# A retention layer feeding a PReLU MLP: another creation order of the early operations

## The chip, the cores and the metric

The kernel runs on one core of a Trainium2 chip. A core has five engines that run side by side and wait for each other through semaphores: TensorE (PE; its weight loads are shown as PEld), VectorE (DVE), ScalarE (ACT), GpSimd (POOL) and SyncE (SP), whose queue here issues the DMA transfers. The metric is the device time of one execution in microseconds (us). Times are medians over runs. The profile is one execution taken by the hardware profiler; its span runs from the first to the last instruction.

## What is computed

```python
def _attn_ref(q, k, v):                      # 8 batches, 8 heads, 576 rows, 64 columns
    scores = scale * np.matmul(q, k.transpose(0, 1, 3, 2))
    gamma = 1.0 - 2.0 ** (-5.0 - np.arange(H, dtype=np.float32))
    rel = pos[:, None] - pos[None, :]
    Dmat = np.where(rel >= 0, gamma[:, None, None] ** rel[None, :, :], 0.0)
    return np.matmul(scores * Dmat[None], v)
...
def _moe_ref(x, w_in, w_out, alpha):         # x is 4608 x 512, w_in 512 x 2048, w_out 2048 x 512
    h = x @ w_in
    g = np.maximum(h, 0.0) + alpha * np.minimum(h, 0.0)
    return g @ w_out
```

The output of the first function, heads side by side, is `x` of the second. The weights arrive as 64-bit words (the kernel reads them as pairs of 32-bit integers) and are converted to float32 on the chip.

## The kernel before

**Retention.** Rows of a batch are cut into 9 chunks of 64. Within a chunk the masked scores are formed; what earlier chunks contribute goes through a state of 64 x 64 per head. The first two batches are worked in *parts* of 4, 4 and 1 chunks over all heads: parts 0, 1, 2 are batch 0, parts 3, 4, 5 are batch 1. A part is loaded (`load_part`: k, q, v rows, 256 KB per 128 rows), q and v are scaled on POOL (`part_scale`, L455), k and q are turned on PE and copied out by ACT (`part_transposes`, L479, L485), scores are formed and masked (`part_scores`, L503, L510), states are summed (`part_states`, L526, L541), carried to the next part on POOL (`part_carry`, L547), and values are formed from scores (L574) and states (L599, in part 0 L615) and copied to the `x` tiles (L631). The one-chunk parts go through `last_part` (L652 turns k and q, L665 to L691 the rest). Later batches are worked as head pairs: `joint_(n)` issues the score and state products of pair n (L913 to L923) together with the values of pair n-1 (L861), and the loads and scalings of the next ones.

**MLP.** `x` stands in 18 blocks of 256 rows, the hidden width in 8 units of 256. A *visit* is a block with four units. The first two visits (8 *cells*: block 0 or 1 with units 0 to 3) run as plain float32 products: `unit_plain` (L1091, then L1097, L1102 for the PReLU) and `second_plain` (L1122). Later visits run on operands split in three pieces each (`split_roll`, `split_w`, `split_g`): `unit_roll` (L1188) and `second` (L1340) in the *rolling steps* s = 0 to 14, each with two units i of two halves f, and from the last blocks on `unit_two` (L1222).

**Weights.** `weights(n)` fetches the next n of the 16 early weight pieces (512 KB each), converts them (ACT L730, L732; DVE L740, L742, L751; POOL L754) and leaves them in the `lx_w` rooms, from which the plain units read them. Unit u reads pieces 4u and 4u+1, its second product pieces 4u+2 and 4u+3. The cells are numbered so that block 0 and 1 take units 0 and 1 first; cells 0 and 1 therefore use pieces 0 to 7. `split_w(i)` later splits piece i into the three planes for the rolling steps (L783, L785, L790).

**Order.** Nothing is issued at once. Every call of `do` or `dma` appends an operation with its engine, an estimated cost, its dependencies and the buffers that it takes. *Creation order* decides which use of a buffer comes before which, and so some dependencies, and breaks ties; PE operations are also picked only from a stretch of 150 in creation order. At the end `dues` works out from behind how late each operation may be, `plan` lists the operations forward, engine by engine, and a loop of 243 random shifts of the due times keeps what `plan` rates best. The instructions are then issued in that planned order, and each engine and queue runs its own in order.

During the first 100 us of the plan at most 1.25 MB of transfers are allowed in flight on SP's queue (`IN_FLIGHT`).

**Unread products.** `fill` (L1405) issues products of the identity into a bank that nobody reads: 5 at the start, 3 more behind part 0's first transposes, and 10 after part 0's values, each float32 product being two records in the trace.

## Time and profile before

| | |
|---|---|
| median of 3 runs | 919.32 us (918.11 to 922.28) |
| span of the profiled execution | 917.4 us |
| instructions | 19097, of which PE 7289 products |
| granted TensorE clock | 1.000 |
| largest group | second products of the rolling steps, L1340, 1392 records in 338.8 us |
| HBM | 74.19 MB read, 32.51 MB written |

A row of the profile names the line, the engine, the operation, the tiles it writes and reads, the shapes and how many instructions are merged. In rows of a timeline the first two numbers are the start in the span and the time to the end of the group; the bracket is the idle time of the engine before the group and what ended it. A matmul's end is modelled and overlaps its successor, so distances are better read from start to start.

### The profile page before, as it was taken

Reading aid. Unit: us, or ns where it says so; the run is one execution under the profiler, and the core shown is the slowest. Engines: PE = TensorE matmul, PEld = TensorE weight load, DVE = VectorE, ACT = ScalarE, POOL = GpSimd, SP = SyncE. Lnnn points to the kernel's source line nnn. Section 1 sums busy time; section 2 is a strip of 40 time slices with the busy share of each in tenths; the row PEclk is TensorE's granted clock in tenths of the full one; section 3 lists DMA queues with packets and bytes.
Section 4 is the critical chain, followed back from the end, with each engine's and each line's share of the span. In section 5 each row is a group of like instructions: output and inputs, shape, how many; then the busy total and the mean of one; then the engine's idle time right before and its main releaser. Section 6 shows DMA issues by size and latency. Waiting matters only on the chain. (4 is left out here: it accounts for less than half of the span.)

```text
span 917.4 us, 19097 instructions
## 1 busy us (share of the span) xinstructions
PE 906.9 (99%) x7289; PEld 737.8 (80%) x7289; DVE 548.0 (60%) x1003; ACT 503.9 (55%) x1010; POOL 520.2 (57%) x461
## 2 busy tenths in 40 slices
PE   7999999999999999999999999999999999999998
PEld 6767688887888888888888888888888888888886
DVE  5786766667677667676757776344444534344343
ACT  4575455646565656565746555537463636364441
POOL 4776746456466665674542244665656656574624
PEclk9999999999999999999999999999999999999999
DMA  9995688977988879895243332212121322211112
GB/s 216 251 235 86 164 189 186 198 178 155 221 192 194 209 166 201 193 189 181 93 138 130 102 125 65 86 57 81 58 89 56 99 73 86 74 64 47 47 46 69
DMA packets 235947, 121.32 MB, mean 132 GB/s; under 512 B 203456, under 2 KB 203728, under 8 KB 235856
## 3 DMA queue, kind: packets, MB, share of 16 engines
q1 hardware_dynamic: 235712, 119.98, 52.1%
q8 instruction: 57, 0.93, 0.4%
q14 instruction: 34, 0.28, 0.1%
q10 hardware_dynamic: 144, 0.13, 0.0%
HBM read 74.19 MB, written 32.51 MB: 116 GB/s over the span
## 5 line engine op out<-in xcount | busy, mean ns | idle before, releaser
L1340 PE MATMUL pso<-w,g 128*128 128x512 f32 x1392 | 338.8, 391 | 0.0
L1340 PEld LDWEIGHTS pso<-w,g 128*128 128x128 f32 x1392 | 258.9, 188 | 55.2 <-POOL g L1267 1.2
L1264 POOL TENSOR_TENSOR g<-ga_all,g 128x512 fp32r<-128x512 f32 x76 | 97.9, 1291 | 130.4 <-ACT g L1260 105.0
L1267 POOL TENSOR_TENSOR g<-g 128x512 fp32r<-128x512 f32 x114 | 147.4, 1294 | 23.7 <-DVE su L1066 5.7
L1188 PE MATMUL psh<-lx_x,w 128*128 128x512 f32 (+1 forms) x360 | 86.6, 379 | 0.0
L1188 PE MATMUL psa<-lx_x,w 128*128 128x512 f32 (+1 forms) x360 | 85.4, 376 | 0.0
L1188 PEld LDWEIGHTS psa<-lx_x,w 128*128 128x128 f32 x360 | 65.1, 188 | 13.1 <-issue 0.4
L1188 PEld LDWEIGHTS psh<-lx_x,w 128*128 128x128 f32 x360 | 64.2, 188 | 12.9
L1260 ACT ACTIVATE g<-ga_all 128x512 fp32r<-128x512 f32 x76 | 47.6, 631 | 43.0 <-PE pso L1340 21.0
L1256 POOL TENSOR_TENSOR g<-g 128x512 fp32r<-128x512 f32 x22 | 28.5, 1296 | 64.0 <-DVE g L1253 38.3
L1264 POOL TENSOR_TENSOR g<-vn,g 128x512 fp32r<-128x512 f32 x25 | 32.4, 1297 | 37.5 <-ACT g L1260 34.9
L1340 PE MATMUL pso<-lx_x,g 128*128 128x512 f32 x216 | 53.5, 390 | 0.1
L1163 POOL TENSOR_TENSOR lx_x<-lx_x 128x512 fp32r<-128x512 f32 x28 | 35.9, 1294 | 26.0 <-DVE lx_x L1160 26.0
L941 DVE SCALAR_TENSOR_TENSOR at<-psa,pf,mask 64x512 f32<-64x512 f32 x48 | 36.0, 749 | 21.1 <-PE psh L861 10.2
L1340 PEld LDWEIGHTS pso<-lx_x,g 128*128 128x128 f32 x216 | 40.4, 188 | 9.0 <-DVE o L1363 0.7
L1262 ACT ACTIVATE g<-ga_all 128x512 fp32r<-128x512 f32 x76 | 47.2, 621 | 0.0
L1358 DVE TENSOR_TENSOR op<-pso,op 128x512 f32<-128x512 f32 x35 | 24.0, 686 | 31.3 <-PE pso L1340 31.2
L1202 ACT COPY ga_all<-psh 128x512 f32<-128x512 f32 (+1 forms) x30 | 16.7, 558 | 39.1 <-PE psh L1188 37.4
L861 PEld LDWEIGHTS psh<-at,vn 128*64 128x64 f32 x864 | 27.9, 137 | 8.7 <-issue 3.6
L1222 PE MATMUL psh<-w,w 128*128 128x512 f32 x144 | 34.6, 389 | 0.0
L1222 PE MATMUL psa<-w,w 128*128 128x512 f32 x144 | 34.6, 389 | 0.0
L754 POOL TENSOR_TENSOR wa<-wa,op 128x512 int32<-128x512 int32 x16 | 21.0, 1311 | 23.1 <-DVE wa L751 19.1
(329 smaller groups left out, 1883.3 us busy)
## 6 DMA issues: line engine op xcount, KB each, us to landing
xk<-x SPq DMA_DIRECT2D x18, 512.0 KB, 3.7
ok<-o SPq DMA_DIRECT2D x36, 256.0 KB, 2.9
op<-ok SPq DMA_DIRECT2D x18, 512.0 KB, 3.9
out_dram<-o SPq DMA_DIRECT2D x35, 256.0 KB, 2.3
x<-xk SPq DMA_DIRECT2D x16, 512.0 KB, 5.6
qx<-in_q_dram SPq DMA_DIRECT2D x96, 72.0 KB, 3.4
kx<-in_k_dram SPq DMA_DIRECT2D x96, 72.0 KB, 3.3
kn<-in_k_dram SPq DMA_DIRECT2D x48, 144.0 KB, 3.4
```

What stands on the lines that cost most here:

```text
L861: nc.tensor.matmul(pv[i].get()[half(h2), (j - js[0]) * C:(j - js[0] + 1) * C], vns[n % 2][:, h2, j], mt.get()[:, h2, j], start=True, stop= ...
L941: nc.vector.scalar_tensor_tensor(out=mt.get()[half(1 - h2), h2, j], in0=fro[x], scalar=pf[x, 1, h:h + 1], in1=mask[x, None, :].to_broadcas ...
L1163: do("POOL", 1.29, lambda h=h, l=l, d=d: nc.gpsimd.tensor_tensor(out=piece(d()), in0=h(), in1=l(), op=ALU.subtract), [(g, 0, n), (g, 1, n) ...
L1188: nc.tensor.matmul(out_of(p), w[:, c0:c0 + P], xp(l, cc), start=(l != 1 and cc == 0), stop=(l > 0 and cc == NCC - 1))
L1222: nc.tensor.matmul(p.get(), w[:, c0:c0 + P], piece(words_of(g)[:, o:o + DM]), start=(l != 1 and cc == 0), stop=(l > 0 and cc == NCC - 1))
L1256: do("POOL", 1.29, lambda: nc.gpsimd.tensor_tensor(out=piece(to.get()[:, 2]), in0=to.get()[:, 0], in1=to.get()[:, 1], op=ALU.subtract), [( ...
L1260: do("ACT", 0.64, lambda: nc.scalar.mul(piece(to.get()[:, 2]), whole(), BELOW), both, [(to, 2)])
L1262: do("ACT", 0.64, lambda: nc.scalar.mul(piece(to.get()[:, 0]), whole(), BELOW * 2.0 ** -12), both, [(to, 0)])
L1264: do("POOL", 1.29, lambda: nc.gpsimd.tensor_tensor(out=piece(to.get()[:, 1]), in0=whole(), in1=to.get()[:, 2], op=ALU.subtract), both + [( ...
L1267: do("POOL", 1.29, lambda: nc.gpsimd.tensor_tensor(out=piece(to.get()[:, 2]), in0=to.get()[:, 0], in1=to.get()[:, 1], op=ALU.subtract), [( ...
L1340: nc.tensor.matmul(a[2 * m + b].get(), piece(g.get()[:, l, f, m * P:(m + 1) * P]), w_piece(u, 2 + f, l), start=(cell["first"] and f == 0 a ...
L1358: do("DVE", 0.69, lambda: nc.vector.tensor_tensor(out=t(), in0=p1.get(), in1=t(), op=ALU.subtract), [(p1, 0)], [tk])
```

## The change

What was a sequence of statements up to the first rolling step becomes a tuple `early` of small steps, called in turn, that also takes in the rolling steps 0 to 3. The loop for the rest starts at step `FIRST = 4` and makes the same calls as before. The same loads, parts, units, weight pieces, splits and joints are created, in another order:

- the 8 unread products at the start and behind the first transposes stand nearer to each other; the 10 ahead of the first plain unit are gone;
- weight pieces are asked for one by one between the steps of the parts; part 2 is loaded ahead of part 1, the alphas ahead of part 0's transposes, the first head pair's rows right after;
- part 0 goes in the order k's transposes, q's transposes, states, scores, values; `last_part(2)` stands ahead of the second products of cell 1;
- `split_w` of the 16 early pieces, all behind `joint_(8)` before, are spread from the middle of part 4 on; cells 4 and 5 exchange their second products; the second product of cell 7 comes after the first rolling half unit;
- block 3 is split ahead of block 2 in `split_roll`;
- dependencies of an operation are kept in creation order (`sorted`) instead of a set's.

```diff
-        op.deps = [d for d in deps if d is not op]
+        op.deps = sorted((d for d in deps if d is not op), key=lambda d: d.n)
...
-    EARLY, JOINTS = 1, {(s, i): 1 for s in range(14) for i in range(2) if (s, i) not in ((0, 0), (8, 1), (10, 1), (13, 0), (13, 1))}
+    FIRST, JOINTS = 4, {(s, i): 1 for s in range(14) for i in range(2) if (s, i) not in ((0, 0), (8, 1), (10, 1), (13, 0), (13, 1))}
...
-    load_part(0, ((0, 0), (1, 0), (1, 1), (0, 1), (2, 0), (2, 1)))
-    bank = banks_of(0)
-    fill(5, 0.43)
-    part_transposes(0, 0, bank)
-    fill(3, 0.43, [next(op for op in ops if op.eng == "PE" and len(op.deps))])
-    part_scale(0, 1)
-    part_transposes(0, 1, bank)
-    part_scores(0, bank)
-    part_scale(0, 2)
-    weights(3)
-    part_states(0, bank)
-    do("DVE", 2.0, tables, (), [(cst, "t")])
-    part_carry(0)
-    part_values(0, bank)
-    fill(10, 0.25, of_pe())
-    weights(1)
-    fetch_x(visits[0])
...
-    load_part(1)
-    bank = banks_of(1)
-    unit_plain(cells[0])
...
-    done.add(8)
-    joint_(8)
-    second_plain(cells[7])
-    for i in range(16):
-        split_w(i)
...
+    bank0, bank1 = banks_of(0), banks_of(1)
+    early = (
+        lambda: load_part(0, ((0, 0), (1, 0), (1, 1), (0, 1), (2, 0), (2, 1))),
+        lambda: fill(5, 0.43),
+        lambda: weights(1),
+        lambda: weights(1),
+        lambda: part_scale(0, 1),
+        lambda: fill(3, 0.43, of_pe()[:1]),
+        lambda: part_scale(0, 2),
+        lambda: load_part(2),
+        lambda: load_part(1),
+        lambda: alpha(),
+        lambda: part_scale(1, 1),
+        lambda: load_kq(8),
+        lambda: part_transposes(0, 0, bank0),
+        lambda: weights(1),
+        lambda: do("DVE", 2.0, tables, (), [(cst, "t")]),
+        lambda: part_transposes(0, 1, bank0),
+        lambda: part_states(0, bank0),
+        lambda: part_transposes(1, 1, bank1),
+        lambda: part_scores(0, bank0),
+        lambda: part_scale(1, 2),
+        lambda: part_values(0, bank0),
+        lambda: fetch_x(visits[0]),
+        lambda: weights(1),
+        lambda: part_scale(2, 1),
+        lambda: part_transposes(1, 0, bank1),
+        lambda: weights(1),
+        lambda: part_scores(1, bank1),
+        lambda: unit_plain(cells[0]),
+        lambda: part_carry(0),
+        lambda: weights(1),
+        lambda: weights(1),
+        lambda: second_plain(cells[0]),
+        lambda: part_states(1, bank1),
+        lambda: part_carry(1),
+        lambda: unit_plain(cells[1]),
+        lambda: part_values(1, bank1),
...
+        lambda: last_part(2),
+        lambda: second_plain(cells[1]),
+        lambda: unit_plain(cells[2]),
+        lambda: unit_plain(cells[3]),
...
+        lambda: split_roll(visits[3]),
+        lambda: split_w(12),
+        lambda: split_roll(visits[2]),
+        lambda: next_joint(),
+        lambda: unit(0, 0, 0),
+        lambda: pump(1),
+        lambda: second_plain(cells[7]),
+        lambda: unit(0, 0, 1),
...
+        lambda: next_split(6),
+    )
+    for step in early:
+        step()
+    land[0] = LAND[1]
+    for s in range(FIRST, last):
+        begin(s)
...
```

In the new list `bank0` and `bank1` are two generators over the same PSUM banks as before, `unit(s, i, f)` makes one half of a rolling unit, `next_split` and `next_joint` call `split_roll` and `joint_`, and `swap` gives the `lx` rooms their second use.

More of the change, by code (lines that the diff above doesn't have):

```diff
@@ L1425 @@
-    fill(10, 0.25, of_pe())
-    weights(1)
-    fetch_x(visits[0])
-    dma(lambda: a16, lambda: moe_alpha.rearrange("(t p) -> t p", p=P), NFC * P * 4, (), [(cst, "al")])
-    aps = Gen(psa[0])
-    do("PE", 0.2, lambda: nc.tensor.transpose(aps.get()[:, 0:NFC], a16, ident[0:NFC, 0:NFC]), [(cst, "al")],
-       [(aps, 0)])
-    do("DVE", 0.1, lambda: nc.vector.tensor_scalar(malpha, aps.get()[:, 0:NFC], -1.0, 1.0,
-                                                   ALU.mult, ALU.add), [(aps, 0)], [(cst, "a")])
@@ L1434 @@
-    load_part(1)
-    bank = banks_of(1)
-    unit_plain(cells[0])
-    weights(2)
-    part_transposes(1, 0, bank)
-    part_scale(1, 1)
-    part_transposes(1, 1, bank)
-    second_plain(cells[0])
-    weights(2)
-    part_scale(1, 2)
-    part_scores(1, bank)
-    part_states(1, bank)
-    unit_plain(cells[1])
-    load_part(2)
-    part_values(1, bank)
-    part_carry(1)
-    fetch_x(visits[1])
-    part_scale(2, 1)
-    part_scale(2, 2)
-    rooms(3)
-    load_part(3)
-    second_plain(cells[1])
@@ L1456 @@
-    unit_plain(cells[2])
-    last_part(2)
-    weights(2)
-    for x in (4, 5):
-        rooms(x)
-    part_transposes(3, 0, bank)
-    part_scale(3, 1)
-    part_transposes(3, 1, bank)
-    second_plain(cells[2])
-    part_scores(3, bank)
-    part_scale(3, 2)
-    part_states(3, bank)
-    part_carry(3)
-    unit_plain(cells[3])
-    part_values(3, bank)
-    load_part(4)
-    weights(2)
-    second_plain(cells[3])
-    part_transposes(4, 0, bank)
-    part_scale(4, 1)
-    part_transposes(4, 1, bank)
@@ L1477 @@
-    unit_plain(cells[4])
-    load_part(5)
-    weights(2)
-    second_plain(cells[4])
-    part_scores(4, bank)
-    part_scale(4, 2)
-    part_states(4, bank)
-    part_carry(4)
-    unit_plain(cells[5])
-    part_values(4, bank)
-    load_kq(8)
-    load_kn(8)
-    load_v(8)
-    weights(2)
-    second_plain(cells[5])
-    part_scale(5, 1)
-    part_scale(5, 2)
-    unit_plain(cells[6])
-    last_part(5)
-    operands(8)
-    load_kq(9)
-    load_v(9)
-    second_plain(cells[6])
-    unit_plain(cells[7])
@@ L1501, with alpha @@
-    done.add(8)
-    joint_(8)
-    second_plain(cells[7])
-    for i in range(16):
-        split_w(i)
+    def alpha():
+        dma(lambda: a16, lambda: moe_alpha.rearrange("(t p) -> t p", p=P), NFC * P * 4, (), [(cst, "al")])
+        aps = Gen(psa[0])
+        do("PE", 0.2, lambda: nc.tensor.transpose(aps.get()[:, 0:NFC], a16, ident[0:NFC, 0:NFC]),
+           [(cst, "al")], [(aps, 0)])
+        do("DVE", 0.1, lambda: nc.vector.tensor_scalar(malpha, aps.get()[:, 0:NFC], -1.0, 1.0,
+                                                       ALU.mult, ALU.add), [(aps, 0)], [(cst, "a")])
@@ L1507, with swap @@
+    def swap():
+        was_in = lxs[0].gen.ops + lxs[1].gen.ops
+        for x in lxs:
+            x.gen = None
+        lxs[:] = lx_slots("x")
+        for x in lxs:
+            Gen(x).before = was_in
     ready_kb = [((kb + 1) * TB - 1) // S for kb in range(NKB)]
-    todo = iter(range(2 * NPAIR + 1, len(pairs) + 1))
+    todo = iter(range(2 * NPAIR, len(pairs) + 1))
+    done.add(2 * NPAIR)
     of = {}
@@ L1610, in take_rooms, with slow, g, begin @@
             lambda f: rows[:, :, f * TB:(f + 1) * TB] if len(cs) == 2 else rows[:, 0, f * TB:(f + 1) * TB])
-    was_in = lxs[0].gen.ops + lxs[1].gen.ops
-    lxs[:] = lx_slots("x")
-    for x in lxs:
-        Gen(x).before = was_in
-    for _ in range(EARLY):
-        joint_(next(todo))
-    land[0] = LAND[1]
-    split_roll(visits[2])
-    last = singles - 1
-    t = 8
-    for s in range(last):
+    last = singles - 1
+    t = [8]
+    plan_of, held_rooms = {}, {}
+    def slow(f):
+        def g(*a):
+            was, land[0] = land[0], LAND[1]
+            f(*a)
+            land[0] = was
+        return g
+    def begin(s):
         some = [visits[kb] for kb in (1 + s, 2 + s) if 2 <= kb <= last]
@@ L1625, with unit @@
         now_cells = {(vis["n"], u): c for vis in some for c in of[vis["n"]] for u in us if c["u"] == u}
-        queue += [now_cells[vis["n"], u] for vis in some for u in us]
+        queue.extend(now_cells[vis["n"], u] for vis in some for u in us)
+        plan_of[s] = sorted(some, key=lambda vis: vis["kb"] % 2), us, now_cells
+    @slow
+    def unit(s, i, f):
         quick[0] = s >= QUICK
-        by_side = sorted(some, key=lambda vis: vis["kb"] % 2)
-        if s == 0:
-            split_roll(visits[3])
@@ L1631 @@
-        for i, u in enumerate(us):
-            cs = [now_cells[vis["n"], u] for vis in by_side]
-            gens, g = take_rooms(cs)
-            for f in range(2):
-                for _ in range(ahead.get(t, 0)):
-                    convert((op_, 0), was, None)
-                t += 1
-                ps = unit_roll(by_side, u, f, True)
-                acts_roll(ps, gens, g, u, f)
-                if f:
-                    for c, ga in zip(cs, gens):
-                        c["ga"] = ga, ga.get
-                    ahead_g()
-                pump(PUMP_R[i][f])
-                if f:
-                    for _ in range(JOINTS.get((s, i), 0)):
-                        joint_(next(todo))
-                if i and f and 3 + s <= last and s:
-                    assert NPAIR * (ready_kb[3 + s] + 1) in done
-                    split_roll(visits[3 + s])
+        by_side, us, now_cells = plan_of[s]
@@ new lines, in unit, with next_split @@
+        cs = [now_cells[vis["n"], us[i]] for vis in by_side]
+        if not f:
+            held_rooms[s, i] = take_rooms(cs)
+        gens, g = held_rooms[s, i]
+        for _ in range(ahead.get(t[0], 0)):
+            convert((op_, 0), was, None)
+        t[0] += 1
+        ps = unit_roll(by_side, us[i], f, True)
+        acts_roll(ps, gens, g, us[i], f)
+        if f:
+            for c, ga in zip(cs, gens):
+                c["ga"] = ga, ga.get
+            ahead_g()
+    @slow
+    def next_split(s):
+        assert NPAIR * (ready_kb[s] + 1) in done
+        split_roll(visits[s])
@@ new lines, in next_joint @@
+    @slow
+    def next_joint():
+        joint_(next(todo))
+    bank0, bank1 = banks_of(0), banks_of(1)
[36 more added lines that the diff above has]
+        lambda: part_values(1, bank1),
+        lambda: rooms(3),
+        lambda: weights(1),
+        lambda: fetch_x(visits[1]),
+        lambda: load_part(3),
+        lambda: rooms(4),
+        lambda: part_scale(2, 2),
+        lambda: last_part(2),
+        lambda: second_plain(cells[1]),
+        lambda: unit_plain(cells[2]),
+        lambda: unit_plain(cells[3]),
+        lambda: rooms(5),
+        lambda: part_transposes(3, 0, bank1),
+        lambda: weights(1),
+        lambda: part_scale(3, 2),
+        lambda: part_states(3, bank1),
+        lambda: load_part(5),
+        lambda: part_scale(3, 1),
+        lambda: load_part(4),
+        lambda: part_transposes(3, 1, bank1),
+        lambda: begin(0),
+        lambda: part_scale(4, 1),
+        lambda: part_carry(3),
+        lambda: weights(1),
+        lambda: weights(1),
+        lambda: weights(1),
+        lambda: weights(1),
+        lambda: part_scale(4, 2),
+        lambda: part_scores(3, bank1),
+        lambda: part_transposes(4, 1, bank1),
+        lambda: part_values(3, bank1),
+        lambda: part_transposes(4, 0, bank1),
+        lambda: part_states(4, bank1),
+        lambda: second_plain(cells[2]),
+        lambda: part_scores(4, bank1),
+        lambda: weights(1),
+        lambda: unit_plain(cells[4]),
+        lambda: split_w(7),
+        lambda: second_plain(cells[3]),
+        lambda: part_values(4, bank1),
+        lambda: load_kn(8),
+        lambda: load_v(8),
+        lambda: weights(1),
+        lambda: operands(8),
+        lambda: part_scale(5, 2),
+        lambda: unit_plain(cells[5]),
+        lambda: second_plain(cells[5]),
+        lambda: split_w(6),
+        lambda: part_scale(5, 1),
+        lambda: split_w(13),
+        lambda: load_kq(9),
+        lambda: load_v(9),
+        lambda: second_plain(cells[4]),
+        lambda: split_w(10),
+        lambda: unit_plain(cells[6]),
+        lambda: next_joint(),
+        lambda: split_w(5),
+        lambda: weights(1),
+        lambda: second_plain(cells[6]),
+        lambda: split_w(2),
+        lambda: part_carry(4),
+        lambda: split_w(1),
+        lambda: split_w(11),
+        lambda: split_w(14),
+        lambda: split_w(9),
+        lambda: split_w(3),
+        lambda: split_w(0),
+        lambda: unit_plain(cells[7]),
+        lambda: last_part(5),
+        lambda: split_w(4),
+        lambda: split_w(8),
+        lambda: swap(),
+        lambda: split_roll(visits[3]),
+        lambda: split_w(12),
+        lambda: split_roll(visits[2]),
+        lambda: next_joint(),
+        lambda: unit(0, 0, 0),
+        lambda: pump(1),
+        lambda: second_plain(cells[7]),
+        lambda: unit(0, 0, 1),
+        lambda: pump(1),
+        lambda: unit(0, 1, 0),
+        lambda: split_w(15),
+        lambda: pump(1),
+        lambda: unit(0, 1, 1),
+        lambda: next_joint(),
+        lambda: pump(1),
+        lambda: begin(1),
+        lambda: unit(1, 0, 0),
+        lambda: pump(1),
+        lambda: unit(1, 0, 1),
+        lambda: next_joint(),
+        lambda: pump(1),
+        lambda: unit(1, 1, 0),
+        lambda: pump(1),
+        lambda: unit(1, 1, 1),
+        lambda: pump(1),
+        lambda: next_joint(),
+        lambda: next_split(4),
+        lambda: begin(2),
+        lambda: unit(2, 0, 0),
+        lambda: pump(1),
+        lambda: unit(2, 0, 1),
+        lambda: pump(1),
+        lambda: next_joint(),
+        lambda: unit(2, 1, 0),
+        lambda: pump(1),
+        lambda: unit(2, 1, 1),
+        lambda: pump(1),
+        lambda: next_joint(),
+        lambda: next_split(5),
+        lambda: begin(3),
+        lambda: unit(3, 0, 0),
+        lambda: pump(1),
+        lambda: unit(3, 0, 1),
+        lambda: next_joint(),
+        lambda: pump(1),
+        lambda: unit(3, 1, 0),
+        lambda: pump(1),
+        lambda: unit(3, 1, 1),
+        lambda: next_joint(),
+        lambda: pump(1),
+        lambda: next_split(6),
+    )
@@ L1651 @@
+    for step in early:
[3 more added lines that the diff above has]
+        begin(s)
+        for i in range(2):
+            for f in range(2):
+                unit(s, i, f)
+                pump(PUMP_R[i][f])
+            for _ in range(JOINTS.get((s, i), 0)):
+                next_joint()
+        if 3 + s <= last:
+            next_split(3 + s)
         if s == X_TWO:
```

## The prediction

> **What bounds the kernel now.** I read the page's busy shares and slices first, then the stages, then single engines inside the first 40 us. The page:

> ```profile
> PE 906.9 (99%) x7289; PEld 737.8 (80%) x7289; DVE 548.0 (60%) x1003; ACT 503.9 (55%) x1010; POOL 520.2 (57%) x461
> ...
> PE   7999999999999999999999999999999999999998
> ...
> DMA  9995688977988879895243332212121322211112
> ```

> TensorE (PE) is busy in every slice but the first. So a reordering can gain only what PE wastes early, or what the order itself costs. The stages of the run (time, PE, weight load, DVE, ACT, POOL busy, clock, DMA share, GB/s):

> ```profile
> 0.00:8.00 8.00, 5.73 (x24) 5.06 (x24) 6.25 (x41) 2.41 (x3) 3.07 (x16) 1.00 0.87 166
> 8.00:16.00 8.00, 5.77 (x205) 4.69 (x205) 3.00 (x8) 1.80 (x4) 4.85 (x6) 1.00 1.13 255
> 16.00:24.00 8.00, 7.57 (x203) 6.77 (x201) 5.03 (x8) 6.88 (x12) 4.29 (x4) 1.00 0.89 234
> 24.00:32.10 8.10, 6.79 (x206) 5.46 (x204) 7.75 (x15) 3.42 (x8) 5.22 (x6) 1.00 0.88 240
> 32.10:100.00 67.90, 67.78 (x952) 47.31 (x951) 52.59 (x94) 42.03 (x80) 48.82 (x43) 1.00 0.78 173
> 100.00:900.00 800.00, 799.85 (x5667) 658.16 (x5659) 465.33 (x828) 445.92 (x904) 449.01 (x386) 1.00 0.49 126
> ```

> Up to 32.1 us PE idles 6.2 us and the DMA engines are full (0.87 to 1.13). After 32.1 us PE idles 0.12 and then 0.15 us. So the end is set by two things: when PE becomes dense, and how much PE time lies behind that point. What makes it dense at 32.1 us, on SyncE's queue, POOL and PE:

> ```profile
> 26.20 0.62 SPq L209 DMA_DIRECT2D w<-in_k_dram  x1
> ...
> w<-in_k_dram SPq DMA_DIRECT2D x1, 128.0 KB, 6.2
> ```

> ```profile
> 30.09 1.04 POOL L455 TENSOR_TENSOR w<-w,tp 64x512 f32<-64x512 f32 x1 [1.23 <-DMA w<-in_q_dram]
> 31.10 1.28 POOL L754 TENSOR_TENSOR lx_w<-lx_w,w 128x512 int32<-128x512 int32 x1
> ```

> ```profile
> 32.12 1.98 PE L1122 MATMUL pso<-lx_w,ga_all 128*128 128x512 f32 x4
> 34.04 0.71 PE L652 MATMUL psa<-ident,w 64*128 64x64 f32 x8
> 34.68 1.98 PE L1122 MATMUL pso<-lx_w,ga_all 128*128 128x512 f32 x4
> ```

> The k rows of part 2 are issued at 26.20 and take 6.2 us: they land at 32.4 us. Weight piece 3 is finished by POOL (L754) at 32.4 us, and the first second product (L1122) starts then. L652, which turns part 2's k and q rows, comes behind it.

> **What the change removes.** Its built order has 10 PE products fewer, and as many instructions on every other queue as before. The 10 are the unread ones at 18.97 us (two records each):

> ```profile
> 1.69 2.50 PE L1405 MATMUL psh<-ident 128*128 128x128 f32 x10 [1.69 <-POOL ident masks.py:199]
> ...
> 18.97 2.61 PE L1405 MATMUL psh<-ident 128*128 128x128 f32 x20
> 23.11 1.13 PE L1091 MATMUL psh<-x,lx_w 128*128 128x256 f32 x4 [0.43 <-POOL lx_w L754]
> ```

> They take 2.54 us. What hides them is the wait for weight piece 0: POOL finishes it at 21.75 + 1.30 = 23.05, and the first plain product (L1091) starts at 23.11 after 0.43 idle. Removing them is worth 0, unless piece 0 came early, then up to 2.5; but the wait for k of part 2 stands behind it, so 0 is taken for both.

> **What it moves before 32 us.** The 25 transfers up to k of part 2 are the same set in another order: v ahead of q in part 0, the alphas third instead of seventh, both q halves of part 1 ahead of its k. They are 6.4 MB, the DMA engines are full, and the in-flight limit on the queue is unchanged, so a transfer lands when the one in its place landed before, and k of part 2 at 32.4 us again. On PE I follow the changed order with the rows of before (scaling on POOL 1.04, weight join on POOL 1.29, the three DVE steps of a piece 2.1, transposes 0.5 per half, a small group of 32 products 1.09, half a plain unit 1.92):
> - The 8 unread products stand together and end about 5.1; the alphas, now ahead of part 0's transposes, land about 5.6. The cost is half a microsecond, covered by the transfers behind.
> - Part 0 and the transposes of part 1 go on at the pace of the landings, to 16 to 18 us.
> - The second state product of part 1 needs v's second half (21.4 us), scaled by POOL. That is queued behind the join of piece 0, which DVE releases about 21.0 (landed 17.4, two steps on ACT behind the copies there, 2.1 on DVE): 21.0 + 1.29 + 1.04 = 23.3, and the products end about 23.9.
> - Half a unit 1.92, values 1.09, the other half 1.92, state values 1.09: 29.9 us.
> - Then comes L652, which in the changed order stands ahead of the second product, and with it all of PE waits for k: 32.4 + 0.1 = 32.5. L652 takes 0.64 and the second product 1.82, so both are done at 35.0. Before, both were done at 34.68.

> So the early part costs +0.35, with an idle stretch of 2.6 us that nothing fills. Bounds: k can land a microsecond sooner (the DMA share is 0.88 in that stage, 12% of 8.1 us); then piece 3 at 32.4 limits and the step is worth -0.45. One transfer later (1.2 us between landings early on): +1.6. I take +0.35.

> **What it moves behind 32 us.** The same products in another order. After 35.0 us the walk meets the landings with little to spare: piece 4 about 34.6 for 35.0, piece 5 about 37.4 for 37.5, piece 7 about 43.1 for 43.3; later pieces by 4 us and more. The work that DVE and ACT have ahead of each plain unit (instructions times the mean of their rows) agrees within 3.3 us with before. Plane splits (L785) are created earlier, but POOL, 72% busy from 32 to 100 us (48.82 of 67.90), takes them. The first head-pair products come about 8 us earlier (82.6 by the walk, 90.6 before); their last v lands at 75.9 before and stands some places further ahead in the changed queue, so still 7 us or more ahead of use. I take 0 for all this, with an upper bound of one POOL join late, +1.3, and a lower one of the 0.27 of idle.

> One thing is counted exactly: how often PE goes from full products to the 64-row ones and back. The rows around one such place (small products stand ahead of 117.07 and from 126.81):

> ```profile
> 117.07 3.01 PE L1188 MATMUL psh<-lx_x,w 128*128 128x512 f32 x12
> 119.92 1.52 PE L1340 MATMUL pso<-w,g 128*128 128x512 f32 x6
> 121.28 2.88 PE L1188 MATMUL psa<-lx_x,w 128*128 128x512 f32 x12
> 124.00 2.88 PE L1340 MATMUL pso<-w,g 128*128 128x512 f32 x12
> 126.81 0.27 PE L913 MATMUL psh<-qT,kT 64*64 64x64 f32 x2
> ```

> Start to start, twelve products take 2.72 among their like (121.28 to 124.00), 2.85 behind small ones (117.07 to 119.92) and 2.81 ahead of them (124.00 to 126.81). A visit to the small ones costs 0.13 + 0.09 = 0.22 us. The order has 52 visits before and 47 after: 5 x 0.22 = -1.1 us.

> **The sum.** +0.35 - 1.1 = -0.75 on a span of 917.4: 916.65. The median shown is 919.32 (918.11 to 922.28), 1.9 above that span; I carry the difference to it: 918.6. Half a per cent, which is what a measurement of this kernel can tell from no change, is 4.6 us: below 914.7 is faster, above 923.9 slower.

> **The rivals.**
> 1. *PE's clock falls in the new idle stretch* (slower than before). The row at 1.69 has 250 ns a product, that at 18.97 has 130: PE starts at half speed. The transposes (L479, four in 1.12 us at 4.17 and 1.06 at 6.36, then 0.66 at 8.11) put the change at about 8 us, after 6.4 us. The clock line says 1.00 throughout, so it does not show this. If the 2.6 us ahead of L652 brought half speed back for as long, PE would lose 3.2 us: 919.32 + 0.35 - 1.1 + 3.2 = 921.8. For it: the removed products filled such a stretch. Against it: after 1.3 us of wait in part 0's values and others of about 1 us, products ran at full speed. It decides if L652's eight records take 1.3 instead of 0.64. [...]
> 2. *The helpers come late* (slower by over 0.5%). DVE is busy 7.75 of 8.1 us from 24 to 32; if a weight chain (2.1 + 1.29) slips whole for pieces 4 or 5 and again for 6 or 7, behind a late transfer, PE waits 2 x 3.4: 919.32 - 0.75 + 6.8 = 925.4. For it: margins of 0.1 to 0.4 us. Against: before, the same engines kept PE dense.
> 3. *The transfers land sooner in the new order.* 12% of the 16 us from 16 to 32 are 1.9; weight pieces and k both come forward, and with the idle 0.27: 919.32 + 0.35 - 1.9 - 1.1 - 0.3 = 916.4. For it: transfers of weights and rows mix differently. Against: the bytes are the same. To be over 0.5% faster it needs 1.7 more, which the rows do not hold but the spread of runs does.
> 4. *That the change doesn't do what it says* is excluded by the order for the products; for the time it is the forecast.

> **Chances.** Forecast 0.50, rival 1 0.14, rival 2 0.13, rival 3 0.23. Of rival 3, 0.12 falls beyond 914.7, with 0.02 of the forecast's edge: faster 0.14. Rival 2 and 0.02 of rival 1: slower 0.15. Same 0.71. The range goes from 914.8 (rival 3 less the 1.2 to 1.6 by which runs lie lower) to 923.0 (rival 1 plus 1.2, leaving rival 2 out). The forecast's own range is 917.0 to 920.5.

> **What would show it.** Right: L652 starts at about 32.5 behind a wait of 2 to 3 us for k of part 2; PE idles under 0.5 us from there to 900; twelve products still take 2.72. Rival 1: records of 250 ns behind the wait. Rival 2: PE waits for POOL L754 between 35 and 45 us. Rival 3: k lands before 31 us. I am wrong if PE is dense well before 32 us, or has waits of microseconds in the rolling steps.

## The result, and the profile after

| | before | after |
|---|---|---|
| median | 919.57 us (918.11 to 922.28, 4 runs) | 924.08 us (922.31 to 925.03, 4 runs) |
| ratio, with its 95% interval | | 1.0046 [1.0026, 1.0065] |
| profiled execution: time, span | 919.3, 917.4 us | 925.03, 923.0 us |
| first rolling product (L1188) starts at | 105.00 us | 109.38 us |
| from there to the end | 812.41 us | 813.57 us |

The changed kernel is 4.5 us slower, outside the range and on the other side of the forecast. The profiled execution of after is the slowest of its four, so its span lies 5.5 above that of before. From the first rolling product on both kernels run the same 5648 product records. So the last two rows split the loss of these two executions without any model: 4.4 us arise ahead of that product and 1.2 behind it. One execution of run 1 below, of 1288 us at a mean granted clock of 0.655, is left out of its median.

The busy shares and slices on the page of after:

```profile
PE 907.8 (98%) x7269; PEld 738.4 (80%) x7269; DVE 548.4 (59%) x1003; ACT 503.6 (55%) x1010; POOL 520.0 (56%) x461
...
PE   7899999999999999999999999999999999999998
PEclk8999999999999999999999999999999999999999
DMA  9997689888988867876335232222221232211112
```

TensorE (PE) is busy for 0.9 us more than before with 20 records fewer, and the first slice of its clock shows an 8. The stages up to 40 us of after (time, PE, weight load, DVE, ACT and POOL busy, clock, DMA share, GB/s) show where:

```profile
0.00:8.00 8.00, 3.79 (x17) 3.50 (x17) 6.35 (x36) 1.28 (x1) 4.17 (x17) 1.00 0.86 165
8.00:16.00 8.00, 6.89 (x116) 6.01 (x116) 2.66 (x12) 2.35 (x4) 4.14 (x5) 0.57 1.27 252
16.00:24.00 8.00, 6.03 (x218) 4.90 (x217) 4.41 (x7) 4.51 (x8) 2.56 (x3) 1.00 0.94 247
24.00:32.10 8.10, 7.79 (x192) 6.34 (x192) 7.09 (x13) 4.79 (x10) 4.66 (x6) 0.79 1.10 252
32.10:40.00 7.90, 6.09 (x87) 4.28 (x86) 6.13 (x11) 5.87 (x12) 5.55 (x5) 1.00 1.05 209
```

Before ran 24, 205, 203 and 206 product records in the first four stages. After ran 17 and 116 in the first two: 96 records are late by 16 us. In the second stage PE is busy for longer than before (6.89 against 5.77) and does little more than half the records, at a granted clock of 0.57. The clock falls again in the fourth stage (0.79). The profiled execution of before had 1.00 in all these stages. The fifth stage, where PE of before idled 0.12 us in 67.9, has 1.8 us of idle.

What PE waited for up to 45 us, in after (engine, tile, line, what ended the wait; us in all, times, longest):

```profile
PE psa L479 <- DVE malpha L1416: 3.2, 1, 3.2
PE pso L615 <- issue: 1.8, 1, 1.8
...
PE psa L599 <- issue: 1.2, 1, 1.2
PE psa L652 <- ACT x L631: 0.6, 1, 0.6
...
PE psa L574 <- issue: 0.3, 1, 0.3
```

The same view of before:

```profile
PE pso L574 <- issue: 1.3, 1, 1.3
PE pso L479 <- POOL w L455: 1.1, 2, 0.7
PE psa L599 <- ACT spy L588: 1.0, 1, 1.0
...
PE psh L599 <- issue: 0.3, 1, 0.3
```

Two kinds of wait stand out. One is new: part 0's first transposes (L479) wait 3.2 us for `malpha`, the DVE step that reads the transposed alphas. The other has no releaser ("issue": PE waited for nothing that the profile shows). It was there before, with 1.6 us in two places, and is 3.3 us in three places now.

**The new wait.** The timeline of after, on PE, DVE and POOL (start, length, then the work, and in brackets the idle time ahead of it and what ended it):

```profile
5.65 0.23 PE L1414 MATMUL psa<-ident,a 16*128 16x16 f32 x1 [0.40 <-DMA a<-in_moe_alpha_dram]
9.11 1.11 PE L479 MATMUL psa<-ident,w 128*128 128x128 f32 x4 [3.23 <-DVE malpha L1416]
...
5.84 0.90 DVE L397 COPY tabk<-th 64x4 f32<-64x4 f32 x1
6.75 1.05 DVE L398 COPY gch<-th 64x4 f32<-64x4 f32 x1
...
8.61 0.36 DVE L403 TENSOR_TENSOR gch<-gch 128x4 f32<-128x4 f32 x2
8.89 0.17 DVE L1416 TENSOR_SCALAR malpha<-psa 128x16 f32<-128x16 f32 x1
...
5.64 2.14 POOL L455 TENSOR_TENSOR w<-w,tp 128x512 f32<-128x512 f32 x2 [2.53 <-DVE pf L393]
```

The alphas land when the prediction said, and their transpose runs at 5.65. It goes into bank `psa`, which part 0's transposes take next, so these wait until DVE has read it. On DVE that read stands behind `tables` (L393 to L403), and runs at 8.89 only. Two of the copies of `tables` take 0.90 and 1.05 us, while POOL's scalings run beside them. In before POOL started these later, and the same copies were done by then:

```profile
5.84 0.17 DVE L397 COPY tabk<-th 64x4 f32<-64x4 f32 x1
6.02 0.16 DVE L398 COPY gch<-th 64x4 f32<-64x4 f32 x1
...
6.99 2.15 POOL L455 TENSOR_TENSOR w<-w,tp 128x512 f32<-128x512 f32 x2 [3.88 <-DMA w<-in_q_dram]
```

**The clock.** The trace's clock records of after have full speed from 4.87 to 8.28, half speed from 8.28 to 15.11, full speed, half speed from 25.35 to 28.76, and full speed to the end. Two equal groups of a plain unit, the first of them for the most part inside the second half-speed stretch:

```profile
26.49 3.10 PE L1091 MATMUL psh<-x,lx_w 128*128 128x256 f32 x8
...
31.30 1.99 PE L1091 MATMUL psh<-x,lx_w 128*128 128x256 f32 x8
```

**The stops without a releaser.** In after they are:

```profile
24.05 0.82 PE L615 MATMUL pso<-g,w 64*32 64x64 f32 x52 [1.83 <-issue]
...
30.10 0.21 PE L574 MATMUL psa<-w,w 64*64 64x64 f32 x1 [0.26 <-issue]
...
35.57 0.27 PE L599 MATMUL psa<-w,w 64*64 64x64 f32 x1 [1.20 <-issue]
```

Counted in PE's own records (products, weight loads and PE's semaphore records together), wherever they occur they stand at 451, 706, 962 or 1218 records, in all the traces taken here: 256 apart to within one record. The page has a queue for them, `q8 instruction: 57, 0.93, 0.5%`: 57 packets of 16 KB. PE of after has 14701 records in its trace, 258 for each packet. The trace's packet records give this (us):

| kernel | packet ended | PE goes on at |
|---|---|---|
| before | 14.51, 30.02 | 15.86 (L574), 31.57 (L599) |
| after | 22.74, 28.58, 34.24 | 24.05 (L615), 30.10 (L574), 35.57 (L599) |

In these PE goes on 1.3 to 1.6 us behind the end of a packet. A block of 256 records is about 128 product records with their weight loads. Of the small ones, 52 took 0.82 us (L615 at 24.05), so a block of them alone would last about 2.0 us; of a plain unit's, 8 take 1.92, so a block lasts 31 us. Taken in order, one to a block, each of the first five packets of the twelve traces started 0.05 to 5.0 us after PE had entered the block before. In after, PE entered the block that begins at L615 at 24.05, the next packet started at 27.45, and the block, with all its waits, lasted 6.07 us. I read the stops as PE waiting for its own instructions, which no record shows: this delay, a packet (0.93 to 1.33 us for the first five of after) and the 1.3 us behind it fit into a block of full products, and do not always fit into a block of small ones. The 10 unread products are 40 records, so taking them out shifts every later boundary by 40 records.

### The profile page after: what moved, and what is told of

It reads as the page before. It is cut to its first block, busy times and chain, and to the rows that moved or that the text cites. A ratio compares the mean times of both kernels' runs of the same rounds, so it can differ in the third digit from the quotient of the medians.

```text
span 923.0 us, 19065 instructions
## 1 busy us (share of the span) xinstructions
PE 907.8 (98%) x7269; PEld 738.4 (80%) x7269; DVE 548.4 (59%) x1003; ACT 503.6 (55%) x1010; POOL 520.0 (56%) x461
## 5 line engine op out<-in xcount | busy, mean ns | idle before, releaser
L1340 PE MATMUL pso<-w,g 128*128 128x512 f32 x1392 | 338.1, 392 | 0.2 <-DVE o L1363 0.2
L1340 PEld LDWEIGHTS pso<-w,g 128*128 128x128 f32 x1392 | 259.0, 188 | 56.1 <-POOL g L1267 1.3
L1188 PE MATMUL psh<-lx_x,w 128*128 128x512 f32 (+1 forms) x360 | 86.7, 379 | 0.1
L1188 PE MATMUL psa<-lx_x,w 128*128 128x512 f32 (+1 forms) x360 | 84.2, 376 | 0.3 <-DVE su L961 0.2
L1188 PEld LDWEIGHTS psh<-lx_x,w 128*128 128x128 f32 x360 | 64.3, 188 | 13.8 <-issue 0.7
L1188 PEld LDWEIGHTS psa<-lx_x,w 128*128 128x128 f32 x360 | 64.9, 188 | 13.1 <-DVE su L961 0.4
L1260 ACT ACTIVATE g<-ga_all 128x512 fp32r<-128x512 f32 x76 | 47.6, 631 | 41.6 <-PE pso L1340 23.3
L1264 POOL TENSOR_TENSOR g<-vn,g 128x512 fp32r<-128x512 f32 x25 | 32.4, 1296 | 38.5 <-ACT g L1260 35.2
L1340 PE MATMUL pso<-lx_x,g 128*128 128x512 f32 x216 | 53.3, 390 | 0.1
L941 DVE SCALAR_TENSOR_TENSOR at<-psa,pf,mask 64x512 f32<-64x512 f32 x48 | 36.0, 749 | 23.0 <-PE psa L920 15.3
L1340 PEld LDWEIGHTS pso<-lx_x,g 128*128 128x128 f32 x216 | 40.4, 188 | 9.0 <-DVE o L1363 0.6
L754 POOL TENSOR_TENSOR wa<-wa,op 128x512 int32<-128x512 int32 x16 | 21.0, 1310 | 25.1 <-ACT vn L1232 6.3
L1222 PE MATMUL psh<-w,w 128*128 128x512 f32 x144 | 34.6, 389 | 0.0
L1222 PE MATMUL psa<-w,w 128*128 128x512 f32 x144 | 34.6, 389 | 0.0
```

The costliest lines, as they stand in the source:

```text
L941: nc.vector.scalar_tensor_tensor(out=mt.get()[half(1 - h2), h2, j], in0=fro[x], scalar=pf[x, 1, h:h + 1], in1=mask[x, None, :].to_broadcas ...
L1188: nc.tensor.matmul(out_of(p), w[:, c0:c0 + P], xp(l, cc), start=(l != 1 and cc == 0), stop=(l > 0 and cc == NCC - 1))
L1222: nc.tensor.matmul(p.get(), w[:, c0:c0 + P], piece(words_of(g)[:, o:o + DM]), start=(l != 1 and cc == 0), stop=(l > 0 and cc == NCC - 1))
L1260: do("ACT", 0.64, lambda: nc.scalar.mul(piece(to.get()[:, 2]), whole(), BELOW), both, [(to, 2)])
L1264: do("POOL", 1.29, lambda: nc.gpsimd.tensor_tensor(out=piece(to.get()[:, 1]), in0=whole(), in1=to.get()[:, 2], op=ALU.subtract), both + [( ...
L1340: nc.tensor.matmul(a[2 * m + b].get(), piece(g.get()[:, l, f, m * P:(m + 1) * P]), w_piece(u, 2 + f, l), start=(cell["first"] and f == 0 a ...
```

## The experiments

The ten runs are timed in rounds beside before, with 12 executions each (5 of run 3). The medians of before were 919.38 (beside runs 1 to 4), 919.66 (5, 6, 8 and 9) and 919.54 (7 and 10). Each kernel has its planned order written out in place of the search; in the traces of runs 2 and 3 DVE, ACT, POOL and the DMA queue work in the same order as in after. No run times the written-out order alone. The last two columns are from one execution each, the profiled one: where the first rolling product starts, and the time from there to the end. For after and run 4 it is the longest of their executions, for run 7 one of the shortest.

| run | what it is | median | ratio to before | first L1188 | rest |
|---|---|---|---|---|---|
| before | | 919.57 | | 105.00 | 812.41 |
| after | | 924.08 | 1.0046 [1.0026, 1.0065] | 109.38 | 813.57 |
| 1 | after, `tables` behind the read of the alphas | 921.37 | 1.0021 [1.0001, 1.0041] | 105.47 | 813.52 |
| 2 | after, 14 unread products in the new wait | 923.88 | 1.0046 [1.0032, 1.0060] | 108.12 | 814.29 |
| 3 | after, 10 unread ahead of part 1's scores | 926.56 | 1.0071 [1.0047, 1.0095] | 110.91 | 813.49 |
| 4 | 1 and 3 together | 923.27 | 1.0034 [1.0021, 1.0048] | 109.77 | 813.38 |
| 5 | before without its 10 unread | 922.85 | 1.0030 [1.0015, 1.0046] | 108.66 | 812.20 |
| 6 | after, alphas created later | 923.80 | 1.0043 [1.0024, 1.0061] | 108.43 | 813.62 |
| 7 | after, the 10 unread created again | 927.37 | 1.0063 [1.0042, 1.0083] | 105.75 | 814.66 |
| 8 | 1, and 11 unread in two early places | 924.18 | 1.0046 [1.0031, 1.0061] | 108.53 | 813.40 |
| 9 | after, 14 and 5 unread in two places | 924.65 | 1.0046 [1.0032, 1.0060] | 107.92 | 813.47 |
| 10 | before, its 10 unread some 2 us later in the work | 919.71 | 1.0005 [0.9985, 1.0026] | 106.05 | 812.03 |

Each execution also has a mean granted clock on record; it leaves out the half speed ahead of the clock's first rise (before has 1.000 in its profiled execution, where the first rise comes at 7.30 us). Where this mean is 1.000, the median is 919.1 us for before (15 of its 87 executions), 918.6 for run 10 (4), 920.2 for run 1 (3), 923.1 for run 2 (2), 922.7 for run 8 (2) and 923.4 for run 9 (4). So the falls of the clock are the smaller part of what runs 2, 8 and 9 lose: without any they still take 3.6 to 4.3 us more than before, and their medians over all executions are only 0.8 to 1.5 higher. All four executions of after have falls (0.994 to 0.996).

**Run 1: the read of the alphas ahead of `tables`.** In the list of operations one number moves (61 is `tables`, 39 the read of the alphas; the rest of the list is left out here):

```diff
-        ... 2, 61, 26, 38, 33, 27, 39, 50, ...
+        ... 2, 26, 38, 33, 27, 39, 61, 50, ...
```

> The changed kernel with its planned order written out and one move: DVE's tables (L393 to L403) are issued behind the read of the alphas' bank (L1416) instead of ahead of it. Theory A (clock): the 3.2 us wait ahead of part 0's first transposes is what let the clock fall at 8.3 us; without it the wait is under 0.6 us, the clock does not fall to half between 8 and 15 us, part 2's transposes with the first second product are done by about 36.5 instead of 39.0 us, and the time is 1.5 to 3 us under the changed kernel's 924.1. Theory B (waits alone, the clock doesn't matter because PE waits for transfers anyway): the wait goes to the next transfers, and the time is within 0.7 us of 924.1.

What PE waited for, in run 1:

```profile
PE pso L479 <- DMA w<-in_k_dram: 1.7, 1, 1.7
PE pso L615 <- issue: 1.1, 1, 1.1
...
PE psa L652 <- ACT x L631: 0.6, 1, 0.6
PE psa L574 <- issue: 0.4, 1, 0.4
```

The wait for `malpha` is 0.27 us, and a wait of 1.7 for k's second half by DMA shows behind it. The clock still falls there, which theory A did not have, but half clock is 3.4 us (8.57 to 11.98) instead of 10.2. The median falls by 2.7 us (2.3 by the ratios, whose intervals overlap from 1.0026 to 1.0041), the start of the rolling steps by 3.9. In this trace 0.5 of the 4.4 us are left ahead of the first rolling product, and 1.1 of the 1.2 behind it. Runs 3 and 4 differ by the same edit, and there all executions with it (922.19 to 925.24) lie below all without it (925.75 to 928.08). So the DVE queue ahead of the shared bank is a cause. The edit puts nothing back.

**Run 2: the clock kept up in the new wait.**

```diff
+    UNREAD = {38: 14}
...
+        for _ in range(UNREAD.get(op.n, 0)):
+            nc.tensor.matmul(unread.get()[:, 0:P], ident, ident, start=True, stop=True)
```

(38 is the alphas' transpose.)

> The changed kernel with 14 unread products behind the alphas' transpose, where PE waits 3.2 us; the wait itself stays. Theory A: the clock stays at full speed through 8 to 15 us, the eight transposes records at 9.1 us take 1.0 instead of 1.9 us, and the time falls by 1 to 2.5 us although nothing waits less. Theory B: no gain (within 0.7 us of 924.1), or a loss where the products outlast the wait.

The clock is full from 5.91 to 22.97, as theory A wanted, and the median is that of after. Two stops without a releaser, 1.38 and 1.43 us, fall into small products, and behind them the clock is half from 22.97 to 29.80. This is theory B. The work that fills the wait keeps the clock up there, and its 56 records (14 products, two product records and two weight loads each) shift the boundaries.

**Runs 3 and 4: ten unread products late, alone and with run 1's edit.** As in run 2, with `UNREAD = {84: 10}` (84 is the last operation ahead of part 1's scores).

> The changed kernel with 10 unread products ahead of part 1's scores (about 20.7 us), the place nearest to where the 10 were before. Theory A: PE's stall of 1.8 us in L615 is filled, the clock does not fall at 25.3 us, half a plain unit takes 1.92 instead of 3.03 us, and the time falls by about 1.5 us, the first slow stretch (8 to 15 us) staying. Theory B: the products stand in the way and cost up to 1 us, or nothing.

> Both the move of DVE's tables and the 10 unread products ahead of part 1's scores. Theory A: no fall of the clock after the first microseconds; part 2's transposes and the first second product are done by 35 to 36 us as before the change, and what is left over the kernel before (919.6) is the 1.3 us lost behind 105 us and less: 920 to 921. Theory B: within 1 us of 924.1.

Neither gains. Run 3 is 2.5 us slower than after, more than either expectation; run 4 is 1.9 slower than run 1, as theory B had it. Stops of 1.62 and 0.91 us come in run 3, of 1.48 in run 4, and half speed once more behind them (a mean clock of 0.83 from 32.1 to 40.0 us in run 3, of 0.67 from 24.0 to 32.1 in run 4). Ten products take 2.6 us of their own (20 records in 2.61 us at 18.97 in before), as much as the loss, so these two runs do not tell a price of the boundaries from a price of the products. They show that the products do not help at that place.

**Run 5: before without the 10 products, nothing else.** (62 is the operation that issues them.)

```diff
     for op in (ops[n] for n in ORDER):
+        if op.n in (62,):
+            continue
```

> The kernel before with its planned order written out, less the 10 unread products at 18.97 us; nothing else is moved. Theory A2 (the clock goes by windows of 3.41 us: in the six traces so far it fell behind every window in which PE was busy 1.87 us or less, and behind none with 2.0 us or more): the window that they fill is left with under 1.9 us of work, the clock falls there, and half a plain unit takes about 3 instead of 1.92 us; 1.5 to 3 us slower than before, 921 to 922.5. Rival (the step of my prediction): they cost and bring nothing, 919.4 within 0.6.

What PE waited for, in run 5:

```profile
PE psa L599 <- issue: 3.1, 1, 3.1
PE psh L1091 <- POOL lx_w L754: 1.7, 1, 1.7
...
PE psa L503 <- issue: 0.9, 1, 0.9
PE pso L574 <- issue: 0.9, 1, 0.9
```

The removal alone costs 3.2 us by the medians (2.8 by the ratio). The wait that was to hide it does hide it: PE waits 1.7 us for weight piece 0 instead of 0.43, and the first plain product starts at 23.37 instead of 23.11. The loss comes 10 us later. The stop at record 1218, 0.28 us in before, is 3.07 here, and the clock is half from 35.03 to 38.44. The expectation had the size nearly right by luck: the window that the products had filled kept its full clock (1.00 from 16 to 24 us).

**Runs 6 and 7: undoing one creation step each, planned anew.**

```diff
-        lambda: alpha(),
...
         lambda: fetch_x(visits[0]),
+        lambda: alpha(),
```

```diff
+        lambda: fill(10, 0.25, of_pe()),
         lambda: fetch_x(visits[0]),
```

> The changed kernel with one creation step back in its old place: the alphas' load, transpose and reader are created behind the load of the first block instead of ahead of part 0's transposes; the planner ran anew. The order that it made has the alphas' transpose behind part 0's second transposes. Theory A2: no wait of 3 us ahead of the first transposes, as in the run with the tables moved: 920 to 922. Rival (the later order decides, the alphas do not): within 0.7 of 924.1.

> The changed kernel with one creation step put back: 10 unread products created behind part 0's values; the planner ran anew. In the order that it made the alphas' transpose stands behind part 0's first transposes and the unread products behind L615 and the k transposes of part 1, as in the kernel before. Theory I with the alphas' wait: both causes are lessened, and what is left is the later order: 920 to 921.5. If the order behind 35 us were the cause of most of the loss: 923 to 924.

In run 6 the 3.2 us wait is gone and the clock is full until 32.87. In its place come waits of 1.3, 0.5, 0.6, 0.7 and 0.6 us in part 0 and the first transposes behind it, a stop of 1.63 us at L599, and half clock from 32.87 to 39.70. The median is that of after, as the rival had it; as planning anew put other waits in the place of the one that went, this does not clear the alphas. Run 7 lies outside both expectations. It has no stop above 0.2 us at all, and its rolling steps start at 105.75; the profiled execution then loses 2.3 us behind that point. Its runs come in two groups, five at 921 to 925 and seven at 927 to 929 us, and the profile is of the lower one. The upper ones have a mean granted clock of 0.994 or 0.996, the lower ones 0.996 to 1.000; what makes the distance of 5 us stays open.

**Runs 8 and 9: choosing where the boundaries fall in after.** `UNREAD = {50: 7, 111: 4}` on run 1, `UNREAD = {38: 14, 111: 5}` on after (50 stands in the wait between the halves of the first transposes, 111 behind part 1's scores).

> The run with DVE's tables moved behind the alphas (921.6), with 7 unread products in the wait that is left between the halves of part 0's first transposes and 4 behind part 1's scores. Theory A2: no window under 2.0 us busy, no fall of the clock after it first rose, and a smaller spread of runs; part 2's transposes at about 32 us still, as k lands at 31 to 32 us; 920.0 to 921.0. Theory B (waits alone): no change, 921.6 within 0.5, or the products' own time more.

> The changed kernel with 14 unread products in the wait for the alphas' reader (which stays) and 5 behind part 1's scores. Theory A2: the clock does not fall after it first rose; what is then left over the run with the tables moved is the wait alone. If the clock was most of the loss: L652 by 33 to 33.5 us and 921.5 to 922.5. If the wait of 3.2 us was most of it: L652 at 34.5 or later and 923 to 924.

Run 8 is 2.8 us slower than run 1, with these stops:

```profile
PE psh L503 <- issue: 2.3, 1, 2.3
...
PE psh L526 <- issue: 1.0, 1, 1.0
PE psh L599 <- issue: 0.9, 1, 0.9
```

They add up to 4.1 us, against 1.5 in run 1. The 11 products take about 2.9 us of their own by my estimate (2.61 us for ten at 18.97 in before), though, so the medians alone could be that, as theory B said. Run 9 has stops of 0.94 and 1.82 us and is as slow as after; its L652 starts at 35.36, where the expectation has it if the wait is most of the loss. In both the clock falls once more, which it was not to do: it is half from 22.37 to 25.78 in run 8 and from 27.66 to 31.08 in run 9. The products that were added shifted the boundaries into other small products.

**Run 10: before, with the same 10 products at another place.** They are left out at 18.97 us and issued behind part 1's scores (130). Here the two readings of their worth differ: if they matter for the wait or the clock at 18.97, moving them costs what removing them does; if they matter for the boundaries that come later, moving them by a few operations costs nothing.

```diff
+        if op.n in (62,):
+            continue
...
+    UNREAD = {130: 10}
```

> The kernel before, with its 10 unread products moved from their place at 18.97 us to behind part 1's scores, where PE waits for weight piece 0 anyway; without them at all it took 922.9. Theory I (instruction supply): in every trace so far PE stops with nothing to wait for at the same counts of its own instruction records (451, 706 or 707, 962 or 963, 1218 or 1219: 256 apart), until 1.3 to 1.5 us after a 16 KB packet of the instruction queue; taking the 40 records of the unread products out moved the stop at 1218 so that it lasted 3.07 instead of 0.28 us. Put back behind the scores, the stop at 706 falls among the scores (0.9 us) but the one at 1218 is where it was: under 0.5 us there, the clock does not fall at 35 us, 919.8 to 921.0. Rival (what counts is that PE was kept at work at 18.97 us, for the clock): no better than without them, 922.5 to 923.5.

The first lines of PE's waits in run 10, without the one at the start of the kernel:

```profile
PE pso L574 <- issue: 2.1, 1, 2.1
...
PE psa L599 <- ACT spy L588: 0.2, 1, 0.2
```

The ratio is 1.0005 [0.9985, 1.0026], the 3.1 us stop at L599 is gone, and this although the clock is half from 17.51 to 20.92, where the products stood before. Run 5 and run 10 differ in these 40 records alone, and by 3.1 us. So what the products are worth does not hang on the wait or the clock at 18.97; it fits the boundaries. They are not all of it: the packet ahead of record 1218 started 4.2 us after PE had entered the block before in run 5, 3.0 in before and 2.0 in run 10, and the stop at that record was 3.07 us in run 5, 0.28 in before, and none is listed in run 10.

No run beats before. Run 10 equals it.

## Why the prediction was wrong, point by point

- **"Removing them is worth 0, unless piece 0 came early."** Failed. The cover was as described (run 5: 0.43 grew to 1.7 us of wait). What the walk did not have is that in these traces PE stops at places 256 of its records apart (3.07 us at record 1218 of run 5), so that products taken out shift these places among all later ones. Taking them out of before cost 3.2 us. How much of after's loss is this term cannot be read off: in after's order other small products meet the boundaries, and putting records back (runs 2, 3, 7, 9) gained nothing there.
- **"The alphas, now ahead of part 0's transposes, land about 5.6. The cost is half a microsecond, covered."** The time of landing is right, the cost is wrong. The walk followed transfers and PE, not the bank that the transposed alphas take and not the queue of the engine that must read them. The wait was 3.23 us, and the clock fell in it, at 8.28. Run 1 shows 2.3 to 2.7 us of the loss to be here, the largest part that a run shows. Two unforeseen terms meet in that wait: `tables` on DVE, and 1.6 us by which two of its copies took longer beside POOL's earlier scalings (0.90 and 1.05 us instead of 0.17 and 0.16).
- **"k of part 2 at 32.4 us again" and L652 behind a wait of 2 to 3 us for it.** It landed at 31.08, sooner, as the third rival had it and near its mark of 31. It did not matter: PE reached L652 at 36.51, 4 us late, and waited 0.6 us for ACT. The idle stretch around which the sum was built does not exist.
- **"The early part costs +0.35."** L652 and the first half of the second product were done at 38.98 (37.16 and 1.82) instead of 35.0: +4.3 against before, over ten times the term and outside its bounds of -0.45 and +1.6. This is the term of the sum that failed, and the first two points of this list are the costs that it put at nothing. The signs named in advance for being wrong (PE dense well before 32 us, long waits in the rolling steps) did not come; of the signs for being right, the wait of 2 to 3 us for k failed, and the waits of PE from 38 to 900 us are 1.3 us instead of under 0.5.
- **"I take 0 for all this"** (behind 32 us). Measured: +1.2 us from the first rolling product to the end, with the same 5648 products. It is in every kernel with the later order (813.4 to 814.7 in nine) and in none with the earlier one (812.0 to 812.4 in three). The upper bound of 1.3 held. Of it, 0.8 lies in the first 48 product records of the rolling steps, which take 6.92 us instead of 6.15; two of them wait there for DVE (L961 for 0.21 us, L941 for 0.05), and where the rest comes from is not shown. No run tests one edit of the later order alone.
- **"5 x 0.22 = -1.1."** There are 47 visits instead of 52. The gain is not in the time: from L652 and the half product to the first rolling product, with the same products in between, before took 70.32 us, after 70.40, and the rest is longer. The new waits there (0.5 us at 74.44 for DVE L541 the longest) outweigh whatever the visits gave.
- **Rival 1**, the clock, was right that it falls and wrong about the place: L652's eight records take 0.65 us, full speed, but the clock fell at 8.28 and at 25.35. Its 921.8 was nearer than the forecast. It was priced by one idle stretch of known length; behind the window from 21.94 to 25.35 in after the clock fell though PE was busy for 1.58 of its 3.41 us, so one wait of 1.83 us (it ended at 24.05) was enough there, where the prediction counted shorter waits as harmless because products ran on at full speed behind 1.3. **Rival 2** is out: between 35 and 45 us PE does not wait for POOL's join (L754) at all.

What is shown: the queue ahead of the shared bank (run 1, and run 4 against 3), the worth of the unread products in before and that it does not lie in the wait that they fill (runs 5 and 10), and the later order's 1.2 us by where the time lies. That the boundaries make this worth is the reading that fits; the stops are read as waits for instructions, not proven. What stays open: how after's own loss divides between stops and half clock, since of the nine stops of over 1.35 us that began at full clock eight were followed by a fall; what decides how late a packet starts; which edit of the later order costs its 1.2 us; and the upper group of run 7.

## What to carry to other kernels

Before a small operation is moved ahead on an engine, look up which buffer it takes, which engine must empty that buffer, and what stands ahead on that engine's queue: a transpose of 0.2 us cost 3.2 us of waiting here. In a kernel with long runs of small products, count instructions as well as time: here what was added or removed shifted the places, 256 records apart, at which PE stopped, so that an edit hidden at its own place cost microseconds far behind it (run 5: a stop of 3.07 us, 10 us later), and padding put in by guess lost more than it won (run 3: 2.5 us slower than after). Split a loss at a point where both kernels have the same work behind them before explaining any of it.
